# First-batch keys and queries loaded by three tokens per partition, patterns copied by transfers, and a new order of work

## The chip, the cores and the metric

The kernel runs on one core of one Trainium2 chip. The metric is the time of one execution on the device in microseconds; the time before is 271.98 us, the median of three runs between 271.74 and 272.3 us. The engines are named as the profile names them: PE (matmul; PEld is its weight load), DVE (VectorE), ACT (ScalarE), POOL (GpSimd), SP (SyncE, which here only issues transfers); 16 DMA engines move the data.

## The reference

Inputs q, k and v have the shape [4, 8, 768, 64] (batches, heads, tokens, width), w_in is [512, 2048], w_out [2048, 512], all fp32. First comes an attention that selects chunks of 32 keys:

```python
k_min, k_max = min and max of k over each chunk of 32 keys          # 24 chunks
ub = np.sum(np.maximum(q * k_min, q * k_max), axis=-1)              # a bound for each query and chunk
ub = np.where(chunk is not in the future, ub, -1e9)
top_chunks = np.argsort(ub, axis=-1)[..., -6:]
mask = (chunk of key in top_chunks) & (query position >= key position)
attn = softmax(np.where(mask, q @ k.T / 8, -1e9));  x = attn @ v    # x: [3072, 512] over all heads
```

Then a dense part on the 3072 tokens: `h = x @ w_in`, `g = h * clip(h + 3, 0, 6) / 6`, and the result is `g @ w_out`, [3072, 512] in fp32.

## The kernel before

The work is cut by batch (four), by half of the tokens (384), and by two pairs of heads: sixteen units of two pairs each, n = 0 to 15. Units 0 to 3 are the first batch. For each unit the keys and queries are put in order (width down the partitions), the chunks' limits are reduced on DVE, PE makes the bounds (`bounds`, L442), DVE takes the six largest of each query and makes a mask of them, and PE multiplies queries and keys (`scores`). ACT takes the exponential, POOL cuts the triangle, and PE multiplies with the values (`values`, tile PVP). When a half of a batch has all its heads, its tokens are turned (XT) and go through the dense part: PE `hidden` (L587, tile HP), ACT and DVE (tiles U and GT), PE `result` (L602, tile OP).

The first batch is treated unlike the others. Its keys and queries come as they lie in memory, a token per partition (`load_quad`); each (pair, half) is turned by PE into PSUM with three fp32 transposes against an identity (`turn`, L375, tiles KT and QT), and copied out by ACT or DVE (`turn_out`). The later batches are loaded in blocks of 32 (`load`, L237) and turned by DVE. In the first batch the mask is a matmul of its own with a pattern tile EB; in the later batches a copy of EB lies beside the keys in the same tile KL, and `beside` makes that copy for six KL buffers and two heads each, on DVE, ACT or POOL, whichever is free.

The order of the instructions on each engine is written out by a planner (`class Plan`). Every step is added with an engine, a length, a rank, the steps it comes after, and the buffers it takes and gives. `order` then plays the program through in time by these lengths, picking on every engine the ready step of the lowest rank, and the program is written in that order; each engine then works strictly in that order on the chip. The table SHIFT moves the rank of single steps by their number. The tables RANK, BEHIND (how long after a step's end others may use it) and GATE (after which landed input each half of a weight matrix is loaded) steer it further. All input loads of the first batch are issued by SP and, in part for unit 0, by ACT; SEQ gives their order: K0 Q0 K1 Q1 Q3 Q2 K2 V1 V0 V2 K3 V3. At most eight transfers (lanes) are under way at once. The weights come through POOL's queue in four parts, WIN in two and WOUT in two (`load_weights`, L316 and L319); a tiny read of the gating input goes before each. In the first 45 us, where the plan leaves PE idle, `occupy` issues bf16 matmuls with no use (L365) into spare columns of the bank of the step just issued, to keep PE at work.

Of the kernel before, what the change touches and what calls it, by code (L numbers as in the profile page):

```python
# [48 lines left out]
class Plan:  # L49
# [5 lines left out]

    BEHIND = dict(PE=0.24, ACT=0.15, DVE=0.15, POOL=0.15, SP=0.3, DMA=0.9, GEN=0.0, WT=1.2)
    COLD = 6.5

# [4 lines left out]
    def add(self, engine, length, rank, run=None, after=(), take=(), give=(), port=False, tiles=None, lock=None):  # L63


        step = dict(lengths=engine if isinstance(engine, dict) else {engine: length}, rank=(rank + SHIFT.get(len(self.steps), 0), len(self.steps)),
                    run=run, told=isinstance(engine, dict), port=port, tiles=tiles, lock=lock, take=take, give=give, then=[])
# [26 lines left out]
    def order(self, **busy):  # L94

        free = {e: busy.get(e, 0.0) for e in self.BEHIND}
        port, tiles, locks = dict(DVE=0.0, POOL=0.0), None, {}
# [17 lines left out]
        while events:  # L115
            now, _, done, own = heapq.heappop(events)
            if done:
                behind(done, own)
                if not own:
                    for held in done["give"]:  # L120
                        held[1] -= 1
                        if not held[1]:
                            self.room[held[0]].append(held[2])
            for e, steps in ready.items():
                if free[e] > now + 1e-9:
                    continue
                for st in sorted(steps, key=lambda x: x["rank"][:1] if e == "DMA" else x["rank"]):
# [4 lines left out]
                    elif self.room_for(st):  # L132
                        steps.remove(st)
                        for held in st["take"]:
                            held[2] = self.take(held[0])
                        out.append(st)
# [11 lines left out]
                        if e == "DMA":  # L148
                            weights = max(free["WT"] - now, 0.0) + sum(x["lengths"]["WT"] for x in ready["WT"])
                            length = min(length / 0.15, weights + max(length - 0.15 * weights, 0.0))  # L150
# [18 lines left out]
def kernel(  # L169
# [36 lines left out]

    def bank(name, shape, dtype=FP32):
        return ps_mix.tile(shape, dtype, name=name, tag=tag("m"))
# [65 lines left out]
    for name, x in (("KS", k), ("QS", q)):  # L274
        for part in range(4):
# [58 lines left out]
    def beside(i, j, e):  # L334

        copy(e, KLS[i][OTHER[j], j, :], EB[OTHER[j], i % 2, :])
# [24 lines left out]
    spare = []  # L361

    def occupy(times):
        for _ in range(times):
            nc.tensor.matmul(spare[-1], lhsT=IDENTB[:], rhs=IDENTB[:, 0:spare[-1].shape[-1]], start=True, stop=True)  # L365

    def turn(st, name, half):

        if st["b"] == 0:
            x = st[name][:, half, :, st["own"], :]  # L370
            T = bank(name[0] + "T", [P, HS + P])
            spare.append(T[:, HS:])
            T = st[name, half] = T[:, 0:HS]
            for t in range(HB):
                nc.tensor.transpose(T[:, t * P:(t + 1) * P], x[:, t, :, :], IDENT32[:])  # L375
# [54 lines left out]
    def bounds(us):  # L430
        for u in us:
            T = bank("UBT", [P, HS + P])
            spare.append(T[:, HS:])
            u["UBT"] = T[:, 0:HS]
# [50 lines left out]
    def scores(st, half, t):  # L485
        SP = st["SP", half, t] = ps_score.tile([P, 2, 512], FP32, name="SPS", tag=tag("s"))
        for jb, q0, n, c0 in PLAN[half][t]:
# [31 lines left out]
    def values(st, half):  # L519
        if (st["b"], half) not in X_tiles:  # L520
            X_tiles[st["b"], half] = xpool.tile([P, HB, DMODEL], BF16, name="Xb", tag=tag("x"))
        T = bank("PVP", [P, HS + P])
        spare.append(T[:, 2 * HB * (D + 1):])
        PVP = st["PVP", half] = T[:, 0:2 * HB * (D + 1)].rearrange("p (j n d) -> p j n d", j=2, n=HB)
# [114 lines left out]
    GATE = dict(I0="V2", I1="I0", O0="I1", O1="O0")  # L639
# [15 lines left out]
    def arrive(engine, issue, length, run, after=(), take=(), parts=1):  # L655
# [3 lines left out]
        for part in range(parts):  # L659
# [6 lines left out]
            if engine == "POOL":  # L666
                issued.append(got)
                got = add("GEN", 1.2, 0, after=[got])
            landed.append(add("WT" if engine == "POOL" else "DMA", length, 0, after=[got], give=lane))
# [4 lines left out]
    def load_input(n, name, after=()):  # L674
# [6 lines left out]
        if n == 0:  # L681
            plan.room[name.lower()].remove(0)
            held_inputs[name, 0][2] = 0
            for i, st in enumerate(two):
                lanes = [hold("lane", 1, 4 * (name == "QS") + 2 * i + j) for j in range(2)]
                for lane in lanes:
                    plan.room["lane"].remove(lane[2])
                there[name, st["pair"], 0] = [add("DMA", 1.0 if name == "KS" else 1.15, i + 2 * (name == "QS") - 10, give=lanes)]
        elif n < 4:
            there[name, two[0]["pair"], half] = there[name, rest, half] = [  # L690
                *arrive("SP", 0.52, 0.6, (load_quad, n, name, x), take=take, parts=3,
                        after=[first_issue[1, name]] if n == 3 else [])]
# [20 lines left out]
    for what in SEQ.split():  # L713
# [5 lines left out]
        else:  # L719
            load_input(n, name)  # L720
            landing[what] = there[name, units[n][0][0]["pair"], units[n][1]], lambda n=n, name=name, at=at: units[n][0][0][name][0:1, units[n][1], at, 3, 0:1]
# [14 lines left out]
    def prepare(n):  # L736
# [11 lines left out]
        for st in two:  # L748
# [3 lines left out]
            for name, f in (("KS", "kf"), ("QS", "qf")):  # L752
# [3 lines left out]
                if first:  # L756
                    m = bank_of[name] = hold("m", 2 if name == "KS" else 1)
                    here = direct[name] = [add("PE", 0.34, r + lead, later(turn, st, name, half), after=here, take=[m], give=used)]
# [232 lines left out]
```

## Time and profile before

| | |
|---|---|
| median of three runs | 271.98 us |
| the profiled execution, as timed | 271.37 us |
| its span, first to last instruction | 269.7 us |
| PE busy | 256.8 us (95%) |
| DVE busy | 209.4 us (78%) |
| ACT busy | 191.6 us (71%) |
| POOL busy | 128.7 us (48%) |
| moved by DMA | 33.71 MB in 122720 packets, 113216 of them under 512 bytes |
| granted clock of PE | 1.000 |

A line of a group names the line of the code, the engine, the operation, the output and input tiles, the shape and the count, then the busy time and the mean of one, and the idle time of the engine before these instructions with what ended it. PE's busy time overlaps itself: a matmul is counted to the end of its way through the array, while the next one has begun. [...]

### The profile page before, as it was taken

The numbers are of one execution on the slowest core, as the hardware profiler recorded it, in microseconds if no ns is written. First come the engines' busy times: TensorE is split into PE (matmuls) and PEld (weight loads), VectorE is DVE, ScalarE is ACT, GpSimd is POOL, SyncE is SP. The second block draws the span as 40 slices with busy tenths as digits, with TensorE's granted clock in tenths as the row PEclk, the third lists the DMA queues.
The fourth block names the chain that finished last, engine by engine and source line by source line (L and its number), as shares of the span: only waits on it lengthen the run. The fifth ranks groups of instructions, "written<-read, shape, count | busy, mean of one in ns | idle before, by whom it ended". The sixth has DMA issues, their size and how long they took to land.

```text
span 269.7 us, 6517 instructions
## 1 busy us (share of the span) xinstructions
PE 256.8 (95%) x2350; PEld 152.7 (57%) x2373; DVE 209.4 (78%) x588; ACT 191.6 (71%) x306; POOL 128.7 (48%) x289
## 2 busy tenths in 40 slices
PE   7997999898999999999999999999999999999994
PEld 4645565654445677644664566654665756555443
DVE  7799898989799997899989999999894424857000
ACT  3589899685527899765984499953998874868021
POOL 4168579533767485559734666752842310200000
PEclk9999999999999999999999999999999999999999
DMA  8999999999948999954995599114103003201122
GB/s 166 219 198 188 190 175 154 176 149 185 212 108 117 127 157 176 186 164 139 150 159 141 157 155 181 40 60 139 39 4 117 5 38 139 58 0 41 39 78 79
DMA packets 122720, 33.71 MB, mean 125 GB/s; under 512 B 113216, under 2 KB 118080, under 8 KB 122688
## 3 DMA queue, kind: packets, MB, share of 16 engines
q1 hardware_dynamic: 117952, 28.71, 62.2%
q0 software_dynamic: 3136, 4.19, 9.5%
q10 hardware_dynamic: 1600, 0.39, 0.7%
q8 instruction: 18, 0.29, 0.6%
q14 instruction: 14, 0.11, 0.2%
HBM read 29.23 MB, written 8.26 MB: 139 GB/s over the span
## 4 chain that ended last, share of the span: by engine, by line
PE 73%; DMA 10%; DVE 8%; SPq 4%; ACT 2%; issue 1%; ACTq 0%; DVEq 0%
PE OP L602 28%; PE HP L587 23%; PE SPS L497 9%; DMA KS<-in_k_dram 8%; PE PVP L530 6%; PE UBT L442 4%; SPq L229 2%; DVE GT L595 2%; PE SPS L494 2%; DMA VS<-in_v_dram 2%; ACT PT L507 1%; PE OP L610 1%; SPq L237 1%; DVE KMA L401 1%; DVE KMA L400 1%
## 5 line engine op out<-in xcount | busy, mean ns | idle before, releaser
L587 PE MATMUL HP<-XT,WIN 128*128 128x384 bf16 x512 | 92.4, 326 | 2.4 <-DVE GT L595 2.3
L507 ACT ACTIVATE PT<-SPS 128x1024 bf16<-128x1024 f32 (+1 forms) x96 | 85.3, 927 | 12.0 <-PE SPS L497 9.9
L602 PE MATMUL OP<-WOUT,GT 128*128 128x512 bf16 x345 | 82.3, 379 | 1.9 <-issue 0.5
L592 ACT ACTIVATE U<-HP,THREE 128x384 bf16<-128x384 f32 x128 | 73.0, 594 | 15.1 <-PE HP L587 8.8
L595 DVE SCALAR_TENSOR_TENSOR GT<-U,HP 128x384 bf16<-128x384 bf16 x128 | 67.2, 545 | 14.9 <-ACT U L592 11.0
L587 PEld LDWEIGHTS <-WIN 128*128 128x128 bf16 x512 | 48.5, 98 | 34.4 <-issue 4.0
L602 PEld LDWEIGHTS <-GT 128*128 128x128 bf16 x368 | 35.1, 98 | 40.2 <-issue 3.7
L512 POOL TENSOR_SCALAR_AFFINE_SELECT PT<-PT 128x256 bf16<-128x256 bf16 x96 | 38.9, 418 | 35.9 <-ACT PT L507 34.9
L497 PE MATMUL SPS<-QLA,KL 128*128 128x384 bf16 (+2 forms) x240 | 36.3, 278 | 0.0
L628 ACT ACTIVATE OT<-OP 128x512 f32<-128x512 f32 x22 | 13.1, 597 | 27.4 <-PE OP L602 27.0
L331 POOL TENSOR_SCALAR_AFFINE_SELECT KL<-KF 64x384 bf16<-64x384 f32 x48 | 23.9, 501 | 14.4 <-DVE KF L387 12.1
L331 POOL TENSOR_SCALAR_AFFINE_SELECT QLA<-QF 64x384 bf16<-64x384 f32 x48 | 24.6, 512 | 12.2 <-DVE QF L387 6.3
L497 PEld LDWEIGHTS <-KL 128*128 128x128 bf16 x240 | 21.7, 98 | 12.8 <-issue 0.6
L530 PEld LDWEIGHTS <-PT 128*128 128x128 bf16 x672 | 23.9, 97 | 3.1 <-issue 0.4
L530 PE MATMUL PVP<-VB,PT 128*128 128x65 bf16 x672 | 25.6, 194 | 0.0
L411 ACT ACTIVATE QR<-QF 128x384 f32<-128x384 f32 x30 | 15.4, 531 | 9.4 <-DVE QF L387 9.3
L542 DVE TENSOR_TENSOR Xb<-PVP,RINV 128x384 bf16<-128x384 f32 x32 | 18.5, 579 | 1.1
L580 POOL COPY XT<-BF 128x384 bf16<-128x384 bf16 x20 | 9.3, 504 | 16.7 <-DMA BF<-BD 16.6
L536 DVE RECIPROCAL RINV<-PVP 128x6 f32<-128x6 f32 x32 | 5.9, 185 | 12.6 <-PE PVP L530 12.2
L387 DVE STREAM_TRANSPOSE KF<-KS 128x384 f32<-128x384 f32 x24 | 13.2, 560 | 1.7 <-DMA KS<-in_k_dram 1.3
L387 DVE STREAM_TRANSPOSE QF<-QS 128x384 f32<-128x384 f32 x24 | 12.8, 555 | 2.0 <-DMA QS<-in_q_dram 2.0
L400 DVE TENSOR_REDUCE KMA<-KF 128x12 f32<-128x384 f32 x24 | 13.1, 545 | 0.4
(80 smaller groups left out, 235.8 us busy)
## 6 DMA issues: line engine op xcount, KB each, us to landing
out_dram<-OT SPq DMA_DIRECT2D x23, 256.0 KB, 2.3
KS<-in_k_dram SPq DMA_DIRECT2D x24, 192.0 KB, 5.5
QS<-in_q_dram SPq DMA_DIRECT2D x24, 192.0 KB, 6.5
VT<-in_v_dram SPq DMA_DIRECT2D x24, 192.0 KB, 4.5
WIN<-in_moe_w_in_dram POOLq DMA_DIRECT2D x2, 1024.0 KB, 9.4
WOUT<-in_moe_w_out_dram POOLq DMA_DIRECT2D x2, 1024.0 KB, 10.1
BD<-BT SPq DMA_DIRECT2D x5, 384.0 KB, 2.4
BF<-BD SPq DMA_DIRECT2D x20, 96.0 KB, 2.3
```

Source lines behind the costliest of these rows:

```text
L331: nc.gpsimd.affine_select(out=to, in_=x, pattern=[[0, n]], compare_op=A.is_ge, fill=0.0, base=0, channel_multiplier=0)
L387: nc.vector.transpose(T[:], st[name][:, st["i"], half * HC:(half + 1) * HC, :].rearrange("p c e -> p (c e)"))
L400: nc.vector.tensor_reduce(out=over, in_=chunks, axis=X_AXIS, op=A.max)
L497: nc.tensor.matmul(SP[:, j, c0:c0 + n], lhsT=KLS[st["pair"] % 6][:, j, jb * P:(jb + 1) * P], rhs=st["QL", half][:, j, at:at + n], start=Tr ...
L507: nc.scalar.activation(PT[:, :, 0:cols], SP[:, :, 0:cols], ACT.Exp, scale=scale)
L512: nc.gpsimd.affine_select(out=PT[:, :, c0:c0 + P], in_=PT[:, :, c0:c0 + P], pattern=[[0, 2], [1, P]], compare_op=A.is_ge, fill=0.0, base=0 ...
L530: nc.tensor.matmul(PVP[:, j, n, :], lhsT=PT[:, j, c0:c0 + P], rhs=st["VB"][:, jb, j, :], start=(jb == 0), stop=(jb == qb))
L542: nc.vector.tensor_tensor(out=to, in0=PVP[:, :, :, 0:D], in1=RINV[:].to_broadcast([P, 2, HB, D]), op=A.mult)
L587: nc.tensor.matmul(HP[:], lhsT=WIN[:, kt, f * P:(f + 1) * P], rhs=g["XT"][:, kt, :, :], start=(kt == 0), stop=(kt == KT_HID - 1))
L592: nc.scalar.activation(U[:], g["HP", f][:], ACT.Relu, bias=THREE[:], scale=1.0)
L595: nc.vector.scalar_tensor_tensor(out=g["GT"][:, f, :], in0=g["U", f][:], scalar=6.0, in1=g["HP", f][:], op0=A.min, op1=A.mult)
L602: nc.tensor.matmul(g["OP", t][:], lhsT=g["GT"][:, f, t * P:(t + 1) * P], rhs=WOUT[:, f, :], start=(f == 0), stop=(f == FT - 1))
```

## The change

1. `load_quad`: three neighbouring tokens go to one partition, so that a piece of a transfer is 3 x 64 fp32 values (768 bytes) where it was one token (256 bytes). A load of one unit's keys or queries is two transfers, one for each pair of heads (192 KB each), where it was three (four for unit 0, of 96 KB). A pair's steps wait for its own transfer alone. Unit 0's second transfer is issued by ACT.
2. `turn`: with three tokens on a partition the columns come out in another order, which a transpose does not mend. Six ordinary fp32 matmuls per turn take their place: for each token t of three and each head j of the pair, 64 columns of data are the stationary operand and the identity is the moving one; the result is written into every third column of 64 partitions.
3. `beside`: the twelve copies of EB become transfers that SP issues, from SBUF to SBUF.
4. The matmuls without use stand ahead of a step, in the bank that the step itself will write, after the bank has come free, up to 24 of them, by the idle time that the plan saw before the step (`occupied`).
5. The planner: other lengths and delays for transfers (`share`, BEHIND, FETCH), WIN's first half gated by V3, WOUT's first half by the keys of the second batch (K4), WOUT's second half by WIN's second half; and a new SHIFT table, by which every engine's order differs.

The diff without SHIFT, which is replaced as a whole, and without the lines that only pass new lengths:

```diff
-            two[0][name] = two[1][name] = src_pool.tile([P, 2, HB, 4, D], FP32, name=name, tag=tag(name.lower()))
-        to, x = two[0][name][:, half], heads(x, two[0]).rearrange("j (n p) d -> p n j d", p=P)[:, half * HB:half * HB + HB, :, :]
-        if n == 0:
-            (nc.scalar if part % 2 else nc.sync).dma_start(to[:, :, part], x[:, :, part])
-        else:
-            nc.sync.dma_start(to[:, part], x[:, part])
+            two[0][name] = two[1][name] = src_pool.tile([P, 2, 4, HB, D], FP32, name=name, tag=tag(name.lower()))
+        own = two[part]["own"]
+        (nc.scalar if n == 0 and part else nc.sync).dma_start(
+            two[0][name][:, half, own], heads(x, two[0])[own, half * HS:(half + 1) * HS].rearrange("j (p t) d -> p j t d", t=HB))
...
-    def beside(i, j, e):
-
-        copy(e, KLS[i][OTHER[j], j, :], EB[OTHER[j], i % 2, :])
+    def beside(i, j):
+
+        nc.sync.dma_start(KLS[i][OTHER[j], j, :], EB[OTHER[j], i % 2, :])
...
-            x = st[name][:, half, :, st["own"], :]
-            T = bank(name[0] + "T", [P, HS + P])
-            spare.append(T[:, HS:])
-            T = st[name, half] = T[:, 0:HS]
+            x = st[name][:, half, st["own"]]
+            T = st[name, half] = bank(name[0] + "T", [P, HS])
             for t in range(HB):
-                nc.tensor.transpose(T[:, t * P:(t + 1) * P], x[:, t, :, :], IDENT32[:])
+                for j in range(2):
+                    nc.tensor.matmul(T[:].rearrange("p (n t) -> p n t", t=HB)[64 * j:64 * j + 64, :, t], lhsT=x[:, j, t, :], rhs=IDENT32[:], start=True, stop=True)
...
-    GATE = dict(I0="V2", I1="I0", O0="I1", O1="O0")
+    GATE = dict(I0="V3", I1="I0", O0="K4", O1="I1")
...
-            made["EB", p % 6] = [add(dict(DVE=0.52, ACT=0.81, POOL=0.85), None, r + RANK["eb"], later(beside, p % 6, j), port=True, after=free.get(("KL", p - 6), []))
-                                 for j in range(2)]
+            made["EB", p % 6] = []
+            for j in range(2):
+                lane = hold("lane")
+                issue = add("SP", 0.42, r + RANK["eb"], later(beside, p % 6, j), after=free.get(("KL", p - 6), []), take=[lane])
+                made["EB", p % 6].append(add("DMA", 0.4, 0, after=[issue], give=[lane], share=0.27))
...
+    def occupied(T):
+        for _ in range(idle.pop(0) if idle else 0):
+            nc.tensor.matmul(T[:, 0:P] if len(T.shape) == 2 else T[:, 0, 0, 0:D], lhsT=IDENTB[:], rhs=IDENTB[:, 0:D if len(T.shape) > 2 else P], start=True, stop=True)
+        return T
...
+        idle[:] = []
+        if step["engine"] == "PE" and step["at"] < 45 and step["idle"] > 0.3 + 0.2 * bool(step["tiles"]):
+            idle[:] = [min(24, int((step["idle"] - 0.1 - 0.2 * bool(step["tiles"])) * 0.8 / 0.058))]
```

More of the change, by code (lines that the diff above doesn't have):

```diff
@@ L27 @@
 SHIFT = {
[18 rows of a table removed]
[16 rows of a table added]
 }
 class Plan:
-    BEHIND = dict(PE=0.24, ACT=0.15, DVE=0.15, POOL=0.15, SP=0.3, DMA=0.9, GEN=0.0, WT=1.2)
+    BEHIND = dict(PE=0.24, ACT=0.15, DVE=0.15, POOL=0.15, SP=0.3, DMA=0.7, GEN=0.0, WT=1.2)
     COLD = 6.5
+    FETCH = 15.3, 1.35
     def __init__(self, **room):
@@ L96, in order @@
         free = {e: busy.get(e, 0.0) for e in self.BEHIND}
-        port, tiles, locks = dict(DVE=0.0, POOL=0.0), None, {}
+        port, tiles, locks, opened = dict(DVE=0.0, POOL=0.0), None, {}, {}
         ready = {e: [] for e in self.BEHIND}
@@ L135, in order @@
                             held[2] = self.take(held[0])
+                        st["idle"] = now - max([free[e], *(opened.get((held[0], held[2]), 0.0) for held in st["take"])])
                         out.append(st)
@@ L274 @@
     for name, x in (("KS", k), ("QS", q)):
-        for part in range(4):
+        for part in range(2):
             load_quad(0, name, x, part)
@@ L667, in arrive @@
                 issued.append(got)
-                got = add("GEN", 1.2, 0, after=[got])
-            landed.append(add("WT" if engine == "POOL" else "DMA", length, 0, after=[got], give=lane))
+                got = add("GEN", 1.0, 0, after=[got])
+            landed.append(add("WT" if engine == "POOL" else "DMA", length, 0, after=[got], give=lane, share=0.1 if length > 1 else 0.18 if run[0] is load_quad else 0.15))
         return landed
@@ L684, in load_input @@
             for i, st in enumerate(two):
[L685 to L688, printed above, removed]
+                lane = hold("lane", 1, plan.lane)
+                plan.room["lane"].remove(plan.lane)
+                plan.lane += 1
+                there[name, st["pair"], 0] = [add("DMA", 1.1 if name == "KS" and i == 0 else 0.65, i + 2 * (name == "QS") - 10, give=[lane])]
         elif n < 4:
-            there[name, two[0]["pair"], half] = there[name, rest, half] = [
-                *arrive("SP", 0.52, 0.6, (load_quad, n, name, x), take=take, parts=3,
-                        after=[first_issue[1, name]] if n == 3 else [])]
+            got = arrive("SP", 0.52, 0.65, (load_quad, n, name, x), take=take, parts=2, after=[first_issue[1, name]] if n == 3 else [])
+            there[name, two[0]["pair"], half], there[name, rest, half] = got[:1], got[1:]
         elif half == 0:
@@ L720 @@
             load_input(n, name)
-            landing[what] = there[name, units[n][0][0]["pair"], units[n][1]], lambda n=n, name=name, at=at: units[n][0][0][name][0:1, units[n][1], at, 3, 0:1]
+            landing[what] = there[name, units[n][0][1]["pair"], units[n][1]], lambda n=n, name=name, at=at: units[n][0][0][name][0:1, units[n][1], 3, at, 0:1]
     vs = hold("gt", 2 * H // 2, 1)
@@ L948 @@
             a = add("SP", 0.37, -2000, later(result_out, g, t, nc.sync), after=[a], take=[lane])
-            add("DMA", 0.75, 0, after=[a], give=[ot, lane])
+            add("DMA", 0.75, 0, after=[a], give=[ot, lane], share=0.4)
         r += RANK["step"]
-    for step in (steps := plan.order(PE=3.7, ACT=4.25, DVE=4.4, POOL=3.2, SP=3.7, DMA=1.6, WT=1.6)):
+    for step in plan.order(PE=3.7, ACT=4.25, DVE=4.4, POOL=3.2, SP=1.9, DMA=1.6, WT=1.6):
         chosen = {}
@@ L954 @@
             chosen.setdefault(kind, []).append(number)
-        spare.clear()
+        idle[:] = []
+        if step["engine"] == "PE" and step["at"] < 45 and step["idle"] > 0.3 + 0.2 * bool(step["tiles"]):
+            idle[:] = [min(24, int((step["idle"] - 0.1 - 0.2 * bool(step["tiles"])) * 0.8 / 0.058))]
         if step["run"]:
             step["run"](*[step["engine"]] if step["told"] else [])
-        if spare:
-            end = step["at"] + step["length"]
-            idle = min(other["at"] for other in steps if other["engine"] == "PE" and other["at"] > step["at"]) - end
-            if end < 45 and idle > 0.25:
-                occupy(min(16, int((idle - 0.2) * 0.8 / 0.058)))
 _INS = ['q', 'k', 'v', 'moe_w_in', 'moe_w_out']
```

34 lines of the change are left out of this document (16 added, 18 removed), and 34 rows, old and new, of the table SHIFT.

## The prediction

> **What bounds the kernel now.** I read the busy times by stage first, then TensorE's instructions in the first stages, then the chain that ended last, then the transfers. The stages (columns: the stretch and its length, busy time and instructions of PE, weight loads, DVE, ACT and POOL, granted clock, DMA share, GB/s):
>
> ```profile
> 0.00:35.60 35.60, 30.60 (x363) 19.32 (x363) 29.86 (x108) 25.82 (x43) 18.90 (x50) 1.00 1.12 191
> 35.60:80.00 44.40, 41.65 (x389) 22.92 (x388) 39.82 (x90) 30.78 (x52) 26.68 (x55) 1.00 1.14 169
> 80.00:266.10 186.10, 184.59 (x1603) 110.47 (x1622) 139.72 (x391) 134.37 (x210) 83.16 (x185) 1.00 0.57 103
> 10.00:15.00 5.00, 4.22 (x48) 3.36 (x46) 4.33 (x18) 3.79 (x8) 1.26 (x4) 1.00 1.29 220
> 122.00:123.00 1.00, 0.95 (x6) 0.41 (x6) 1.00 (x3) 0.54 (x2) 0.93 (x4) 1.00 0.67 182
> ```
>
> After 80 us PE is busy for 184.59 of 186.1 us: nothing to win there but by fewer matmuls. Earlier its busy time flatters, since a matmul's modelled duration overlaps the next one's. So I count matmuls and price them by their spacing where they run back to back. The counts, up to the first dense matmul at 35.6 us and up to 80 us:
>
> ```profile
> L494 PE MATMUL SPS<-MT,EB 64*128 64x384 bf16 (+2 forms) x56 | 7.4, 276 | 2.6 <-ACT PT L507 2.0 <-DVE MT L472 0.5
> L494 PE MATMUL SPS<-KL 64*128 64x384 bf16 (+2 forms) x56 | 6.6, 273 | 0.0
> L375 PE MATMUL QT<-IDENT,QS 128*128 128x128 f32 x24 | 4.3, 300 | 0.3 <-DMA QS<-in_q_dram 0.3
> L375 PE MATMUL KT<-IDENT,KS 128*128 128x128 f32 x24 | 4.3, 315 | 0.5 <-DMA KS<-in_k_dram 0.5
> L442 PE MATMUL UBT<-QF,KMA 64*32 64x384 f32 x32 | 4.0, 495 | 0.1
> L442 PE MATMUL UBT<-QR,KMA 64*32 64x384 f32 x32 | 3.9, 486 | 0.1
> L530 PE MATMUL PVP<-VB,PT 128*128 128x65 bf16 x78 | 3.1, 194 | 0.0
> ```
> ```profile
> L587 PE MATMUL HP<-XT,WIN 128*128 128x384 bf16 x128 | 23.4, 326 | 2.2 <-DVE GT L595 2.1
> L602 PE MATMUL OP<-WOUT,GT 128*128 128x512 bf16 x42 | 9.9, 379 | 0.6 <-DVE GT L595 0.4 <-issue 0.2
> L530 PE MATMUL PVP<-VB,PT 128*128 128x65 bf16 x168 | 6.3, 194 | 0.0
> ```
>
> The spacings, from the chain that ended last (start, length, what) and from the timeline of PE:
>
> ```profile
> 11.87 0.54 SPq L243
> ...
> 13.04 4.84 DMA VS<-in_v_dram
> 17.90 0.56 DVE VB L255
> ...
> 33.92 0.78 PE XTP L551 x12
> 34.70 0.98 PE SPS L494 x16
> ...
> 38.38 0.91 PE PVP L530 x30
> ...
> 71.74 0.86 PE OP L602 x4
> 72.61 1.45 PE UBT L442 x32
> 74.22 4.26 PE OP L602 x19
> ...
> 139.56 3.90 PE HP L587 x24
> ```
> ```profile
> 10.31 0.87 PE L375 MATMUL QT<-IDENT,QS 128*128 128x128 f32 x6
> ...
> 16.60 0.85 PE L442 MATMUL UBT<-QF,KMA 64*32 64x384 f32 x8
> ...
> 17.27 0.82 PE L442 MATMUL UBT<-QR,KMA 64*32 64x384 f32 x8
> ```
>
> Useful PE time up to 35.6 us: 112 x 0.061 (0.98/16) = 6.8 for the first batch's scores, 16 turns of three transposes x 0.43 (0.87/2) = 6.9, four bounds x 1.5 = 6.0, 78 x 0.030 = 2.4, 12 x 0.065 = 0.8: 22.9. So 12.7 us of this stage hold no useful matmul. From 35.6 to 80: 128 x 0.1625 = 20.8, 42 x 0.215 = 9.0, the remaining 90 of PVP 2.7, and some 6.6 for the rest of the scores (48 x 0.061), two joint bounds (2 x 1.45) and 12 turns of tokens (0.8): 39.1, so 5.3 are empty. Together 18 us, and only there can this change win.
>
> What holds PE in those stages: the chain runs through SP's issues to V's transfer (13.04), and from 17.90 through DVE to 28 us. DVE is busy 29.86 of the first 35.6 us, ACT 25.82; of the idle rest, 5.7 and 9.8, some 1.3 and 4.2 lie before anything has landed, so 4.4 and 5.6 count.
>
> **The change, part by part.**
>
> *Loads.* The first batch's K and Q (3.1 MB) go in pieces of 768 bytes for 256. Near 10 us only 256-byte pieces move: 220 GB/s at a share of 1.29, or 171 per unit of share. At 122 us it is the words fetched back (96 KB over 32 partitions and four groups, 768 bytes a piece): 182 at 0.67, or 272. At 0.63 of the engine time per byte, 3.1 MB cost some 9.0 us instead of 14.3: an estimate of 5.3 us of transfer time freed, between 0 (if the piece size isn't what counts) and that. SP issues 18 of these loads ahead of the first V (11.87); there will be 12 if V keeps its place, at 0.54 each 3.2 us sooner; the bytes ahead of V would allow 4.6. I take V 3.2 us earlier. It doesn't become 3.2 us of time: next in line is DVE, with those 4.4 idle us, and nothing takes its reductions away. The gain lies between 0 and 4.4; I take the middle, 2.2.
>
> *Turns.* Three fp32 transposes become six fp32 matmuls of 64 columns. The bounds show what an ordinary fp32 matmul costs: each stands twice in the trace (x64 for 32 in the code), and a group with four column tiles moves 384 columns in 0.33 us per step (17.27 - 16.60, two steps), so 128 columns take 0.11. If the two halves of a turn run side by side as the bounds' column tiles do, a turn is six steps, 0.66 + 0.1, or 0.33 us more than now; 16 of them 5.3 us. Otherwise it is twelve steps, 1.42, and 15.8 us more in all. Nearest is the bounds' row: paired. PE's 12.7 empty us (3.4 before the first turn) cover it except where a turn is itself waited for: the first unit's last K and last Q, 0.7 us. Ends: 0 and 2.6 (eight turns).
>
> A rule of the Trainium skill speaks against this part: "TensorEngine Tiling" (Key Properties) says that a change of tiling mode drains the array, and each turn is now a 128x64 island among 128x128 work. The chain shows it once: bounds at 72.61 end at 74.06, the next OP begins at 74.22, so 0.16 us; by the rule 16 turns cost some 2.6 us more, of which the two turns on the path would be 0.3, and the forecast would be 269.2.
>
> *Patterns.* Twelve copies leave three engines (busy, mean, idle before):
>
> ```profile
> L257 POOL TENSOR_SCALAR_AFFINE_SELECT KL<-EB 64x768 bf16<-64x768 bf16 x6 | 5.1, 844 | 2.7 <-DVE IDENTB L301 1.7 <-PE SPS L494 0.8
> ...
> L253 ACT COPY KL<-EB 64x768 bf16<-64x768 bf16 x3 | 2.5, 822 | 0.0
> L255 DVE COPY KL<-EB 64x768 bf16<-64x768 bf16 x3 | 1.4, 462 | 0.0
> ```
>
> 9.0 us of engine time. Four of the twelve stand before 6 us in the timeline, in idle time; two of ACT's stand at 31.3 and 36.3 us among exponentials that PE waits for (0.82 each). I take 0.3, ends 0 and 1.6. In exchange SP gets 12 issues (6.5 us against 8 x 0.54 = 4.3 saved) and the DMA engines 1.2 MB, 3.4 us at the 768-byte rate (182/0.67 x 1.29 = 350 GB/s), 5.4 at 220. So the freed transfer time is given back by the time the second batch is loaded. They aren't needed before its scores at 79.9 us, which hides them; without that cover they would delay the second batch's loads by those 3.4 to 5.4 us.
>
> *Weights and order.* The weight loads now form a file, each issued when the one before has landed:
>
> ```profile
> 24.89 1.00 POOL L316 DMA_DIRECT2D WIN<-in_moe_w_in_dram  x1
> ...
> 34.53 0.77 POOL L316 DMA_DIRECT2D WIN<-in_moe_w_in_dram  x1
> 45.54 0.93 POOL L319 DMA_DIRECT2D WOUT<-in_moe_w_out_dram  x1
> 55.94 0.92 POOL L319 DMA_DIRECT2D WOUT<-in_moe_w_out_dram  x1
> ```
>
> With the new gates the first WOUT half waits for K of the second batch (issued by 27.9 us), so it follows the second WIN half by one issue; the last half follows that WIN half's landing, about 45.5 instead of 55.94. Both WOUT halves then share the engines: complete between 56 and 65.5 us (ten for one half each, side by side or in line), against 66 now. So OP matmuls can fill PE up to 10 us sooner, at least 0. Of the 5.3 empty us of that stage I take a third, 1.7, with ends 0 and 5.3. WIN's first half, moved from V2 to V3, waits for a later transfer in a shorter queue: V3 is last of the first batch, and 4.6 us sooner it comes about when V2 does now. Cost 0.
>
> *Fillers.* The 42 matmuls without use now go in front of a step in its own bank, up to 24 x 0.056 = 1.3 us at a place. Where data come sooner than the plan thinks, they delay the step. I take 0.4 lost, ends 0 and 2.
>
> Sum: 2.2 - 0.7 + 0.3 + 1.7 - 0.4 = 3.1 us off the profiled execution's 271.37 us (span 269.7). That lies 0.6 below the median of 271.98, so the forecast for the median is **268.9 us**.
>
> **The rivals.**
>
> *Hidden anyway.* DVE and ACT set the first 35.6 us, V lands sooner and waits, and the turns take back the rest. For it: DVE has no gap over 0.2 us from 17.9 to 25 us in the chain. Against: ACT has 5.6 idle us there. Gain 0.6 (the patterns and a little of the weights): 271.4.
>
> *Both holes close.* DVE's 4.4 and half of the second stage's 5.3, less 0.7: 6.3 off, 265.7.
>
> *The second batch starves (slower).* With weight loads back to back, the 128-byte loads of K and Q get what is left. For it: the timeline of SP already shows one unit's four Q issues held for 13.23 us beside the first WIN half.
>
> ```profile
> 27.98 13.23 SPq L237 DMA_DIRECT2D QS<-in_q_dram  x4
> ```
>
> Against: 96 OP matmuls belong to the first batch, of which 54 are left at 80 us, 11.6 us of PE work, and the gain of 3.1 uses part of it. It decides from 8.5 us of delay to the second batch's Q; each further us costs one. Were the eight loads from 41 us on put off until 57, they would run 13 us late and cost 4.5: 273.4. "DMA: Bandwidth & Descriptors" of the Trainium skill (Queues, rings and completion order) has each DMA engine take its queues in turn by whole packets; the 13.23 us agree with a small share for the small pieces.
>
> *The turns don't pair (slower).* 15.8 us more PE time against 9.3 empty ones: 6.5 over, 275.4. The bounds' row speaks against it.
>
> **How the numbers follow.** Forecast 48 in 100, own range 267.0 to 270.8 (its parts at half and at one and a half). Both holes 12, hidden 17, starving 16, no pairs 7. A change of 0.2% (0.54 us) is about what can be told here. Faster: 48 + 12 + 9 of the hidden case = 69; same 7 of it; slower 16 + 7 + 1 = 24. From 266.0 to 273.8 leaves out the unpaired case, a quarter of the starving one and half of the closed holes, some 17 in 100.
>
> **What the changed profile would show.** KS and QS issues of 192 KB each with about 3 us to landing and GB/s above 260 before 12 us; first V issue near 8.5 us; 192 fp32 matmuls in the turns, pairs starting within 10 ns, 0.75 us a turn; no KL<-EB on POOL, ACT or DVE and 12 issues on SP; the first HP at about 34 instead of 35.68; the last WOUT issue near 44; empty PE time under 15 us before 80. The prediction is wrong if HP's start hasn't moved, if a turn takes over 1 us, or if PE waits for KF or QF of the second batch between 60 and 85 us.

## The result and the profile after

The changed kernel takes 270.86 us (median of 19 runs, 269.63 to 272.19) where the kernel before, run beside it, takes 272.47 us (19 runs, 271.19 to 274.07): a ratio of 0.9933, 95% interval 0.9913 to 0.9953. That is 0.7% faster, a small change, but the interval leaves out 1. The forecast was 268.9 us and a faster kernel. The profiled execution took 270.71 us, its span is 269.0 us; against the profiled execution of before (271.37) it is only 0.7 us shorter, since that one lies 1.1 us under its median of this day.

The stages of the kernel after (columns as in the prediction), cut at its first dense matmul, at 80 us, and three short stretches:

```profile
0.00:34.40 34.40, 31.59 (x466) 21.48 (x466) 27.84 (x105) 24.01 (x41) 17.64 (x47) 1.00 1.03 212
34.40:80.00 45.60, 45.39 (x415) 25.35 (x417) 40.74 (x99) 33.84 (x57) 22.71 (x51) 1.00 1.13 185
80.00:265.40 185.40, 181.55 (x1588) 108.38 (x1602) 136.66 (x380) 131.78 (x209) 85.21 (x187) 1.00 0.56 102
5.00:10.00 5.00, 5.00 (x94) 4.83 (x94) 3.59 (x9) 3.98 (x9) 2.19 (x4) 1.00 1.11 326
80.00:120.00 40.00, 37.32 (x373) 23.87 (x375) 33.94 (x96) 30.63 (x45) 26.13 (x57) 1.00 0.99 143
84.00:96.00 12.00, 11.31 (x142) 7.76 (x141) 8.92 (x23) 10.24 (x13) 7.33 (x18) 1.00 1.14 134
```

The same stretches of the kernel before:

```profile
5.00:10.00 5.00, 5.00 (x49) 3.48 (x49) 3.24 (x9) 2.03 (x5) 0.98 (x2) 1.00 1.27 215
80.00:120.00 40.00, 39.51 (x398) 25.23 (x410) 35.65 (x108) 33.66 (x50) 24.04 (x55) 1.00 1.07 156
84.00:96.00 12.00, 11.89 (x106) 7.21 (x105) 11.16 (x38) 10.94 (x15) 8.03 (x19) 1.00 1.40 139
```

The first loads do what was forecast of them: 326 GB/s at a DMA share of 1.11 between 5 and 10 us, against 215 at 1.27. That is 294 GB/s per unit of share against 169, or 0.58 of the engine time per byte where the forecast had 0.63. The new thing is in the last rows. After 80 us, where the kernel before had PE busy for 39.51 of 40 us, it is now busy for 37.32, and DVE for 8.92 of the 12 us from 84 on, where it was 11.16.

PE's groups after, the turns up to 34.4 us and the dense part from there to 80 us:

```profile
L377 PE MATMUL KT<-IDENT,KS 128*64 128x128 f32 x96 | 6.7, 289 | 0.2 <-DMA KS<-in_k_dram 0.2
L377 PE MATMUL QT<-IDENT,QS 128*64 128x128 f32 x96 | 6.2, 275 | 0.0
...
L586 PE MATMUL HP<-XT,WIN 128*128 128x384 bf16 x128 | 22.0, 326 | 0.0
L601 PE MATMUL OP<-WOUT,GT 128*128 128x512 bf16 x63 | 14.3, 379 | 0.2 <-issue 0.2
```

192 matmul records are turns, 12 for each of the 16; and 63 OP matmuls stand before 80 us where there were 42, which is 21 x 0.215 = 4.5 us of work done sooner. The chain that ended last shows the price of a turn (x12), and what PE and DVE hang on after 83 us (start, length, what):

```profile
7.97 0.66 PE KT L377 x12
...
34.47 1.41 PE HP L586 x8
...
63.01 0.21 PE OP L601
...
84.64 0.60 ACT OT L627
...
85.25 0.33 SPq L633
...
88.22 5.51 DMA KS<-in_k_dram
...
93.81 0.59 DVE KF L389
```

A result tile is scaled by ACT (OT), SP issues its store (L633), and only then the keys behind it in SP's queue (L246), which DVE must turn (KF). The timeline of SP shows the stop, after and before:

```profile
76.64 8.95 SPq L633 DMA_DIRECT2D out_dram<-OT  x3
85.68 3.75 SPq L246 DMA_DIRECT2D KS<-in_k_dram  x4
```
```profile
76.55 6.40 SPq L634 DMA_DIRECT2D out_dram<-OT  x2
83.05 3.59 SPq L237 DMA_DIRECT2D KS<-in_k_dram  x4
```

Three stores instead of two stand directly ahead of the third batch's keys, and SP stands still from 80.14 to 85.25 us for the last of them. So the keys are issued 2.6 us later than before, while PE arrives sooner. The list of waits of 83 to 118 us shows what that costs DVE, of after and of before (total us, times, longest):

```profile
DVE KF L389 <- DMA KS<-in_k_dram: 3.3, 2, 2.4
```
```profile
DVE KF L387 <- DMA KS<-in_k_dram: 0.6, 1, 0.6
```

To see where time is won and lost I add up PE's useful matmuls by the time they start, at the prices of the prediction (turns and matmuls of no use left out; all of it is 239.7 us). It is worked out from all rows of each trace; a few OP matmuls have no record and are counted by their weight loads. Its last two columns belong to experiments below.

| us of useful PE work by | before | after | keys first | keys first, casts on POOL |
|---|---|---|---|---|
| 35 us | 14.7 | 15.3 | 14.6 | 14.8 |
| 80 us | 54.7 | 59.5 | 58.5 | 58.9 |
| 100 us | 74.8 | 77.9 | 77.8 | 78.2 |
| 120 us | 94.5 | 95.7 | 97.8 | 98.4 |
| profiled execution | 271.37 | 270.71 | 268.22 | 267.76 |

After is 0.6 us ahead at 35 us, 4.8 at 80, and only 1.2 at 120: 0.6 from the first stage (loads, turns and order together), 4.2 from the second, and 3.6 given back. These are single executions. With the keys first the program is the same as after up to 70 us, and yet its execution stands 0.7 us lower at 35 and 0.9 at 70 us (48.8 against 49.7): so early differences under 1 us are at the edge of what one execution tells. From 80 to 120 us the columns do 39.8, 36.2, 39.3 and 39.5 us of work, and that difference is far outside it.

### The profile page after: what moved, and what is told of

It reads as the page before. It is cut to its first block, busy times and chain, and to the rows that moved or that the text cites. A ratio compares the mean times of both kernels' runs of the same rounds, so it can differ in the third digit from the quotient of the medians.

```text
span 269.0 us, 6720 instructions
## 1 busy us (share of the span) xinstructions
PE 258.5 (96%) x2466; PEld 155.2 (58%) x2484; DVE 205.2 (76%) x582; ACT 190.0 (71%) x305; POOL 125.6 (47%) x284
## 4 chain that ended last, share of the span: by engine, by line
PE 73%; DVE 8%; DMA 7%; ACT 4%; SPq 3%; issue 1%; POOL 1%; ACTq 0%; DVEq 0%; POOLq 0%
PE OP L601 24%; PE HP L586 23%; PE SPS L498 6%; DMA KS<-in_k_dram 5%; PE PVP L529 5%; PE UBT L442 5%; PE SPS L495 3%; DVE GT L594 3%; ACT PT L508 3%; PE QT L377 2%; PE KT L377 2%; SPq L246 2%; PE OP L609 1%; DVE KF L389 1%; DMA BD<-BT 1%
## 5 line engine op out<-in xcount | busy, mean ns | idle before, releaser
L508 ACT ACTIVATE PT<-SPS 128x1024 bf16<-128x1024 f32 (+2 forms) x96 | 84.5, 927 | 11.6 <-PE SPS L498 7.9
L586 PE MATMUL HP<-XT,WIN 128*128 128x384 bf16 x512 | 90.1, 326 | 1.3 <-DVE Xb L541 0.8
L601 PE MATMUL OP<-WOUT,GT 128*128 128x512 bf16 x350 | 83.4, 379 | 1.2 <-issue 0.3
L591 ACT ACTIVATE U<-HP,THREE 128x384 bf16<-128x384 f32 x128 | 71.6, 594 | 8.1 <-PE HP L586 4.2
L586 PEld LDWEIGHTS <-WIN 128*128 128x128 bf16 x512 | 48.8, 98 | 32.6 <-issue 1.3
L513 POOL TENSOR_SCALAR_AFFINE_SELECT PT<-PT 128x256 bf16<-128x256 bf16 x96 | 39.6, 423 | 51.5 <-ACT PT L508 50.7
L498 PE MATMUL SPS<-QLA,KL 128*128 128x384 bf16 (+2 forms) x240 | 35.5, 278 | 0.1
L340 POOL TENSOR_SCALAR_AFFINE_SELECT KL<-KF 64x384 bf16<-64x384 f32 x48 | 24.1, 504 | 8.3 <-DVE KF L389 6.7
L529 PE MATMUL PVP<-VB,PT 128*128 128x65 bf16 x672 | 26.3, 193 | 1.2 <-POOL PT L513 1.1
L413 ACT ACTIVATE QR<-QF 128x384 f32<-128x384 f32 x29 | 14.5, 525 | 10.4 <-DVE QF L389 8.5
L541 DVE TENSOR_TENSOR Xb<-PVP,RINV 128x384 bf16<-128x384 f32 x32 | 18.5, 579 | 1.1
L579 POOL COPY XT<-BF 128x384 bf16<-128x384 bf16 x20 | 9.7, 523 | 14.9 <-DMA BF<-BD 14.8
L266 POOL TENSOR_SCALAR_AFFINE_SELECT VB<-VT 128x768 bf16<-128x768 f32 x12 | 10.8, 908 | 6.4 <-DMA VT<-in_v_dram 4.3
```

Of the source, the lines that this page charges most:

```text
L340: nc.gpsimd.affine_select(out=to, in_=x, pattern=[[0, n]], compare_op=A.is_ge, fill=0.0, base=0, channel_multiplier=0)
L413: nc.scalar.activation(QR[:], QF[:], ACT.Relu)
L498: nc.tensor.matmul(SP[:, j, c0:c0 + n], lhsT=KLS[st["pair"] % 6][:, j, jb * P:(jb + 1) * P], rhs=st["QL", half][:, j, at:at + n], start=Tr ...
L508: nc.scalar.activation(PT[:, :, 0:cols], SP[:, :, 0:cols], ACT.Exp, scale=scale)
L513: nc.gpsimd.affine_select(out=PT[:, :, c0:c0 + P], in_=PT[:, :, c0:c0 + P], pattern=[[0, 2], [1, P]], compare_op=A.is_ge, fill=0.0, base=0 ...
L529: nc.tensor.matmul(PVP[:, j, n, :], lhsT=PT[:, j, c0:c0 + P], rhs=st["VB"][:, jb, j, :], start=(jb == 0), stop=(jb == qb))
```

## The experiments

Ratios are to the kernel before, run beside each; the changed kernel's is 0.9933. The medians of the kernel before beside the experiments lie between 272.58 and 273.31 us, so differences in us against 270.86 are uncertain by up to 0.8 us.

### The third batch's keys before the store

```diff
-    for step in plan.order(PE=3.7, ACT=4.25, DVE=4.4, POOL=3.2, SP=1.9, DMA=1.6, WT=1.6):
+    steps = plan.order(PE=3.7, ACT=4.25, DVE=4.4, POOL=3.2, SP=1.9, DMA=1.6, WT=1.6)
+    number = [step["rank"][1] for step in steps]
+    store = steps.pop(number.index(1126))
+    steps.insert([step["rank"][1] for step in steps].index(400) + 1, store)
+    for step in steps:
```

Step 1126 is the third of those stores, step 400 the last of the four key loads.

> The changed kernel with one result's store, for which SP stands still from 80.1 to 85.25 us, moved behind the four key loads of the third batch that stand behind it. If the gain that PE had at 80 us (4.8 us of work ahead of the kernel before) is lost up to 115 us because DVE waits for these keys, the loads are issued near 80 us, the waits of DVE for KS (3.3 us) go, and 1.5 to 3 us come back: 268 to 269.4. If it is lost because the dense work that filled PE there has been used up earlier, the time doesn't move by more than 0.5 us.

Measured: 268.42 us (267.6 to 268.68), ratio 0.9838 [0.9806, 0.987], faster than both kernels. Its SP timeline and its stretch from 80 to 120 us:

```profile
76.57 4.77 SPq L633 DMA_DIRECT2D out_dram<-OT  x2
81.43 3.69 SPq L246 DMA_DIRECT2D KS<-in_k_dram  x4
```
```profile
80.00:120.00 40.00, 39.91 (x436) 24.83 (x415) 36.63 (x103) 33.81 (x51) 28.73 (x62) 1.00 1.05 153
```

The keys go out 4.25 us sooner, PE is busy for 39.91 of 40 us, and DVE's wait for KS is no longer in the list. From 80 to 120 us it does 39.3 us of useful work, where after did 36.2. One instruction's place in one queue was worth 2.4 us: this cause is shown.

### The loads by 256-byte pieces again

```diff
-        own = two[part]["own"]
-        (nc.scalar if n == 0 and part else nc.sync).dma_start(
-            two[0][name][:, half, own], heads(x, two[0])[own, half * HS:(half + 1) * HS].rearrange("j (p t) d -> p j t d", t=HB))
+        to, x = two[0][name][:, half], heads(x, two[0])[:, half * HS:(half + 1) * HS].rearrange("j (t p) d -> p j t d", t=HB)
+        for t in ((0, 1), (2,))[part]:
+            (nc.scalar if n == 0 and part else nc.sync).dma_start(to[:, :, t], x[:, :, t])
...
-                    nc.tensor.matmul(T[:].rearrange("p (n t) -> p n t", t=HB)[64 * j:64 * j + 64, :, t], lhsT=x[:, j, t, :], rhs=IDENT32[:], start=True, stop=True)
+                    nc.tensor.matmul(T[:].rearrange("p (t n) -> p n t", t=HB)[64 * j:64 * j + 64, :, t], lhsT=x[:, j, t, :], rhs=IDENT32[:], start=True, stop=True)
```

> The changed kernel with the first batch's keys and queries in 256-byte pieces again (one token per partition, three transfers a unit); order, turns and everything else stay as changed. If the larger pieces pay through earlier inputs, as the forecast has it, the time rises by 2 to 4 us over the changed kernel's 270.86, V's first issue moves 3 us later and the first dense matmul to 36 or 37 us. If DVE and ACT hide the transfers anyway, the time stays within 0.6 us.

Measured: 278.27 us (277.82 to 279.25), ratio 1.0208 [1.0178, 1.0238], 7.4 us over after, more than the most that the loads' term allowed (4.4). PE's longest wait, and its stretches:

```profile
PE KT L377 <- DMA KS<-in_k_dram: 4.2, 2, 3.9
```
```profile
5.00:10.00 5.00, 4.02 (x60) 3.04 (x62) 2.30 (x6) 2.85 (x6) 1.01 (x2) 1.00 1.36 218
10.00:15.00 5.00, 1.07 (x16) 0.83 (x14) 0.56 (x1) 0.00 (x0) 1.64 (x2) 0.67 1.36 218
15.00:20.00 5.00, 5.00 (x52) 3.33 (x50) 1.96 (x5) 2.48 (x5) 0.51 (x1) 0.65 1.10 200
```

218 GB/s again, and with the order kept PE and DVE stand nearly still from 10 to 15 us (1.07 and 0.56 us busy), since each works strictly in the written order and the next instruction in line waits for its data. The granted clock was 0.67 and 0.65 in these two stretches on top. So this prices "late data in an order drawn for early data", not the part alone.

### Loads and turns of before, in the order of after

```diff
-        own = two[part]["own"]
-        (nc.scalar if n == 0 and part else nc.sync).dma_start(
-            two[0][name][:, half, own], heads(x, two[0])[own, half * HS:(half + 1) * HS].rearrange("j (p t) d -> p j t d", t=HB))
+        to, x = two[0][name][:, half], heads(x, two[0])[:, half * HS:(half + 1) * HS].rearrange("j (t p) d -> p t j d", t=HB)
+        for t in ((0, 1), (2,))[part]:
+            (nc.scalar if n == 0 and part else nc.sync).dma_start(to[:, t], x[:, t])
...
-                for j in range(2):
-                    nc.tensor.matmul(T[:].rearrange("p (n t) -> p n t", t=HB)[64 * j:64 * j + 64, :, t], lhsT=x[:, j, t, :], rhs=IDENT32[:], start=True, stop=True)
+                nc.tensor.transpose(T[:, t * P:(t + 1) * P], x[:, t, :, :], IDENT32[:])
...
```

> The changed kernel's order, gates, patterns by SP and fillers, with the loads in 256-byte pieces and the three fp32 transposes of the kernel before. Loads alone as before took 278.27. If the two parts add up, the turns' 5.3 us come off: 273. If with late inputs PE has room for the dearer turns, they cost less there: 276 to 278. Against 270.86 it says what loads and turns are worth together in this order; the forecast made it 1.5 us.

Measured: 276.81 us (276.12 to 277.57), ratio 1.0142 [1.0114, 1.017]. Loads and turns are as before (a unit's load is three transfers, for unit 0 too); order, patterns, gates and fillers are new, and it is 3.9 us slower than the kernel before. So these without the new loads and turns are a loss; the order is good only with the arrivals that it was drawn for.

### Both kernels without their SHIFT tables

The edit is `SHIFT = {}` in each.

> The changed kernel with an empty SHIFT table, so that its order is the planner's plain one by ranks. To be read against the kernel before with an empty table, which runs beside it. Theory: the parts of the change (loads, turns, patterns by SP, gates) are themselves worth 1 to 3 us, and the rest of what undoing one of them cost (5.5 to 7.4 us) is that the tuned order had been drawn for them: both kernels lose 2 to 8 us without their tables, and this one is 1 to 3 us ahead of the other. Rival: a part is worth in any order what undoing it cost, and then this one is 5 us or more ahead. Second rival: the parts are worth nothing and the new table alone earned the 1.6 us: this one is level with the other or behind it.

> The kernel before with an empty SHIFT table. Theory: 2 to 8 us over the kernel before, a ratio of 1.007 to 1.03, and 1 to 3 us over the changed kernel with an empty table; by the rival 5 us or more over that; by the second rival level with it or under it.

Measured: after 280.5 us (279.93 to 281.3), ratio 1.0286 [1.0245, 1.0326]; before 280.42 us (276.88 to 282.85), 1.031 [1.0219, 1.0401]. The medians are level, but those of before differ in clock: 276.88 us at a granted clock of 1.000, 278.74 at 0.994, 282.09 at 0.986, 282.85 at 0.988. At the full clock after took 279.93 and 280.02, some 3 us more than the one such run of before. So the second rival holds, level or behind. Where it is lost shows in PE's busy time from 80 to 120 us, of after and of before:

```profile
80.00:120.00 40.00, 34.44 (x336) 20.81 (x335) 31.38 (x96) 30.78 (x49) 23.47 (x52) 1.00 1.03 143
```
```profile
80.00:120.00 40.00, 39.57 (x416) 24.74 (x415) 37.14 (x113) 31.78 (x48) 24.48 (x57) 1.00 0.98 146
```

Counted as in the table, after is some 5 us of useful work ahead at 80 us here too, and some 2 us behind at 120. So the parts do gain before 80 us in the plain order as well, and more than that gain is lost behind it. DVE's wait for the third batch's keys isn't among the waits there; the most that PE waits there is 2.3 us, for POOL (PT). What is behind that loss stays open, and so does the price of the parts apart from the table.

### Turns twice

```diff
-            for t in range(HB):
+            for t in [*range(HB), *range(HB)]:
```

> The changed kernel with each turn's matmuls made twice (the same result written again): 192 fp32 matmuls more, 16 x 0.66 = 10.6 us of PE in the first 30 us. If the turns are mostly hidden in PE's empty time, as the forecast has it, only what doesn't fit into some 5 empty us shows: 4 to 6 us more than 270.86. If the turns are the chain at the start, as the changed kernel's chain reads (turn after turn from 4.0 to 9.9 us), nearly all of it shows: 8 to 11 us more.

Measured: 281.18 us (280.95 to 282.19), ratio 1.0317 [1.0288, 1.0347], 10.3 us over after. The work added is 192 matmuls, 16 x 0.66 = 10.6 us:

```profile
L377 PE MATMUL KT<-IDENT,KS 128*64 128x128 f32 x192 | 13.2, 300 | 0.3 <-DMA KS<-in_k_dram 0.3
L377 PE MATMUL QT<-IDENT,QS 128*64 128x128 f32 x192 | 11.5, 274 | 0.0
```

Nearly all of it shows: no empty PE time takes up more turning.

### Turns at half the price

```diff
+            flat = st[name][:, half, st["own"]].rearrange("p j t d -> p (j t d)")
             for t in range(HB):
-                for j in range(2):
-                    nc.tensor.matmul(T[:].rearrange("p (n t) -> p n t", t=HB)[64 * j:64 * j + 64, :, t], lhsT=x[:, j, t, :], rhs=IDENT32[:], start=True, stop=True)
+                nc.tensor.transpose(T[:].rearrange("p (n t) -> p n t", t=HB)[:, :, t], flat[:, t * P:(t + 1) * P], IDENT32[:])
```

> The changed kernel with its loads and its order, but three 128-column fp32 transposes per turn, as before, over the wrong columns (the heads and tokens of a pair come out mixed, so the selection and the result are of other data; the amount of work is the same otherwise). A turn falls from 0.66 to 0.33 us of PE. If a turn's time lies on the path from start to first dense work, as doubling it showed (10.6 us of work added cost 10.3), 16 x 0.33 = 5.3 us go: about 265.6. If the first half of a turn's cost is hidden, as the forecast has it, only 0.7 us go: 270.2.

Measured: 269.91 us (268.11 to 271.25), ratio 0.9885 [0.9828, 0.9941]. Its four runs differ by the granted clock: 268.11 us at 1.000, 269.81 at 0.991, 270.01 at 0.992, 271.25 at 0.987. With less turning PE runs empty for a while, and in three of the four its clock was lower; the profiled one shows both:

```profile
20.00:25.00 5.00, 2.42 (x37) 1.63 (x33) 4.93 (x20) 4.12 (x7) 4.07 (x9) 0.91 0.94 153
25.00:30.00 5.00, 5.00 (x68) 2.62 (x64) 3.20 (x8) 3.15 (x4) 1.59 (x5) 0.75 1.22 211
```

At the full clock half the turning is worth 270.86 - 268.11 = 2.7 of 5.3 us, by a single run; with the lower clock, by the median, 1.0. As far as that one run tells, the dearer turns cost about 2.7, at the far end of the term's 0 to 2.6.

### Turns without a change of tiling mode

The same edit, with `nc.tensor.matmul(..., lhsT=flat[:, t * P:(t + 1) * P], rhs=IDENT32[:], start=True, stop=True)` in place of the transpose: PE's time as in after, in full 128x128 tiles.

> The changed kernel with three ordinary 128-column fp32 matmuls per turn over the wrong columns (result of other data, as in the run with transposes): the same 0.66 us of PE, but no change of tiling mode around a turn. If a change of mode costs the 0.16 us that one place of the chain before shows, 16 turns are 2.6 us cheaper: 268.3 where all of it is on the path. If it costs nothing here, 270.9 within 0.5.

Measured: 271.10 us (270.14 to 272.49, 8 runs), ratio 0.9938 [0.9918, 0.9958], that of after. 16 turns that no longer change the tiling mode bring nothing here (the two ratios differ by 0.0005, 0.1 us). "TensorEngine Tiling (Array Packing)" of the Trainium skill (Key Properties) has a change of tiling mode drain the array. The 2.6 us that the prediction weighed by that rule aren't there.

### Patterns copied by POOL

```diff
-        nc.sync.dma_start(KLS[i][OTHER[j], j, :], EB[OTHER[j], i % 2, :])
+        copy("POOL", KLS[i][OTHER[j], j, :], EB[OTHER[j], i % 2, :])
```

> The changed kernel with the twelve pattern copies on POOL, at the same places in the order, instead of SP's transfers. If the copies cost something because engines are short of time, 12 x 0.84 = 10 us more on POOL show as 0.3 to 1.6 us of time. If POOL has room where they now stand (8 to 13 us and 67 to 74 us), nothing changes within 0.5 us, and SP's queue is 6 us shorter.

Measured: 276.39 us (275.83 to 276.55), ratio 1.0131 [1.0106, 1.0155], 5.5 us over after and outside both expectations. PE's longest wait after 36 us and the chain:

```profile
PE UBT L442 <- POOL KMA L405: 2.9, 1, 2.9
```
```profile
83.65 0.20 POOL KMA L405
...
83.90 0.83 PE UBT L442 x4
...
89.54 0.60 ACT OT L627
90.16 0.33 SPq L633
...
90.58 0.38 SPq L246
...
93.04 5.58 DMA KS<-in_k_dram
```

Eight of the copies, 0.82 us each, stand at 65 to 80 us on POOL, the limits (KMA) behind them, PE's bounds (UBT) behind these, then the result tile, the store, and the third batch's keys, issued 4.9 us later than in after. The chain thus runs through the same store; how much of the 5.5 us that is isn't measured. The copies of the kernel before stood at 3.9 to 49.5 us on three engines, and what they cost there isn't measured by this either.

### Weights by the gates of before

```diff
-    GATE = dict(I0="V3", I1="I0", O0="K4", O1="I1")
+    GATE = dict(I0="V2", I1="I0", O0="I1", O1="O0")
```

> The changed kernel with the gates of the weights as before (WIN's first half after V2, WOUT's halves each after the part before them); the planner draws up the order anew with the same ranks. If the earlier WOUT is what fills PE between 35 and 80 us, WOUT's last issue moves from 43 to about 53 us, PE has some 1.7 us more empty time before 80 us, and the time rises by 1 to 3 us. If order and early inputs are all, it stays within 1 us.

Measured: 277.82 us (275.61 to 277.89), ratio 1.0159 [1.0117, 1.0202]. That is more than either expectation had. The planner drew another order for these gates, so the 7 us are of gates and order together. Useful PE work by 80 us is 57.4, 2.1 less than in after. It doesn't price the gates.

### Without the matmuls of no use

```diff
-        for _ in range(idle.pop(0) if idle else 0):
+        for _ in range(0):
```

> The changed kernel without its matmuls of no use. The trace shows nine of them, 0.5 us in all. By the prediction's term they cost 0.4 us where data come sooner than the plan thinks: then this is 0.2 to 0.6 us faster than the changed kernel, a ratio to before near 0.992. Rival: they keep the granted clock up in the first 40 us, and without them the clock in the rows falls and the time is over 1 us longer, a ratio over 0.997. If neither, they cost and bring nothing: within 0.2 us.

Measured: 270.52 us (270.24 to 271.73), ratio 0.9918 [0.9881, 0.9956]. That can't be told from no change: they cost 0.3 us or nothing. The granted clock was 0.999 or 1.000 in five of the six runs without them (0.992 in one), so they don't keep it up.

### Keys first, and two casts from ACT to POOL

```diff
+        if step["rank"][1] in (271, 129):
+            step["engine"] = "POOL"
```

> The changed kernel with the store put behind the third batch's keys (as in the run before that did this), and two casts of the first batch's values, which stand at about 22 us on ACT, given to POOL at the same places of the order; nothing else differs. Theory: what is left in the first 35 us is ACT's time, since PE waits there some 1.1 us for exponentials and ACT spends 2 x 0.53 us on these casts among them; the gain then stays, because nothing after 80 us takes it back any more: 0.3 to 0.8 us less than with the keys first alone, a ratio to before of 0.981 to 0.983. Rival: POOL's casts of 0.54 us delay the triangles behind them, which the values' matmuls wait for, and the two cancel: a ratio of 0.984 or more. Either way the ratio should stay under 0.990; over that, the gain from putting the keys first was not real.

Measured: 267.40 us (267.09 to 267.76), ratio 0.9804 [0.9772, 0.9836], the fastest here. In its first 36 us PE waits 0.9 us for a mask (DVE MT) where with the keys first alone it waited 1.2 us for exponentials, and the table has it 0.4 us ahead of that run at 80 us and 0.6 at 120. The intervals of the two overlap; the sign is likely, the size isn't settled.

## Why the prediction was right and wrong

*The sign and its places held.* Transfers of 768 bytes go faster, V is issued at 7.35 us (forecast near 8.5), a turn is six steps and 0.66 us, the first dense matmul starts at 34.47 (about 34) and the last WOUT half is issued at 43.12 (about 44). PE's waits before 80 us shrink. Empty PE time before 80 us fell under the 15 us that were forecast: 59.5 us of useful work and 10.6 of turns leave 9.9. Two signs were met in part: the first loads landed after 3.1 to 4.9 us (about 3), and the closest starts within a turn are 6 or 7 ns apart in half of the cases and 17 or 18 in the others (within 10). The median is 2.0 us over the forecast, inside the wide range (266.0 to 273.8) and 0.06 us over the range of its main case (267.0 to 270.8).

*Loads and turns, 2.2 - 0.7 = 1.5.* PE is 0.6 us ahead at 35 us in the profiled execution, and level in that with the keys first: less than half of the 1.5. The step that failed is "PE's 12.7 empty us ... cover it": the turns at half price say 2.7 us at the full clock (one run), not 0.7, and turns made twice added nearly their whole price. Empty time summed over a stage isn't cover, since part of it lies where PE waits for DVE and ACT, and each turn has its place in a chain. That the loads then gave some 3 us gross is worked out from the 0.6 and the 2.7, not measured.

*Weights and order, 1.7.* The second stage gave 4.2, so the upper end (5.3) was nearer than the third that I took: OP matmuls did fill PE, 63 against 42 by 80 us. How much of it is the gates and how much the order stays open.

*Patterns, 0.3.* Not measured as such. That the second batch's scores hide them held: PE's waits name no KL<-EB.

*Fillers, 0.4.* 0.3 or nothing: the size fits, but it can't be told from zero. Only nine of them are in the changed kernel's trace, 42 in that of before.

*"After 80 us ... nothing to win there".* This is the step that missed the time. It is true of winning and was taken for "nothing to lose"; the sum ended at 80 us. PE was full there as long as the third batch's keys came in time (DVE waited 0.6 us for them). The kernel after reaches that point 4.8 us sooner with the keys 2.6 later, and gives back 3.6 by 120 us. Putting the keys first returns 2.4 us of it.

*Luck.* The time lies in the range because two errors work against each other: 4.8 us gained by 80 us where the sum had 3.1, and 3.6 lost behind it where the sum had nothing. That 268.42 us with the keys first is so near the 268.9 of the forecast is luck as well, since the terms of the first two stages were off by 0.9 and 2.5 us in opposite directions.

*The rivals.* By the time alone, 1.6 us gained lies between the 0.6 of "hidden anyway" and the 3.1 of the forecast. That rival comes near in the first stage, which gained 0.6 us, but it has nothing like the 4.2 us of the second. The starving rival had the kind of wait, but looked for it one batch too early, and in bandwidth instead of in the order of one queue. SP was in fact held 20.60 us over three key issues of the second batch (from 34.44 us, beside the weights), and PE still waited for none of that batch's keys or queries between 60 and 85 us.

## What to carry to other kernels

When work moves ahead, look behind the stage that gains: what arrives just in time there can arrive late afterwards, and an engine that is full before the change may not stay full after it. In a queue that issues strictly in order, a store that waits for an engine holds every load behind it; find the long row of that queue's timeline and see what stands after it. Taking one part out of a kernel whose order was tuned for it measures the order too, not the worth of the part: undoing the loads costs 7 us in the tuned order, while all the parts together bring no shorter time in the plain one.

## What the runs showed of the hardware

The granted clock answered the same idle time in different ways. PE ran no matmul from about 10.5 to 14.4 us both with the 256-byte pieces and with the loads and turns of the kernel before in the new order; these stretches are of the first and of the second:

```profile
11.00:12.00 1.00, 0.00 (x0) 0.00 (x0) 0.00 (x0) 0.00 (x0) 1.00 (x2) 0.84 1.37 219
12.00:13.00 1.00, 0.00 (x0) 0.00 (x0) 0.00 (x0) 0.00 (x0) 0.39 (x1) 0.50 1.36 217
...
17.00:18.00 1.00, 1.00 (x12) 0.46 (x12) 0.30 (x1) 0.75 (x2) 0.00 (x0) 0.50 1.28 225
18.00:19.00 1.00, 1.00 (x12) 0.31 (x8) 0.00 (x0) 0.71 (x2) 0.51 (x1) 0.75 0.87 171
```
```profile
12.00:13.00 1.00, 0.00 (x0) 0.00 (x0) 0.00 (x0) 0.00 (x0) 0.42 (x1) 1.00 1.36 217
```

In the first the clock was halved at about 11.7 us (0.84 is two thirds of that microsecond at 1.00 and the rest at 0.50), some 1.2 us after the last matmul, and stayed so until about 18.5 us, 4 us after work had come back; in the second it never fell. "TensorE: Matmul & The Clock Gate" of the Trainium skill (Part 1) has half the clock after at least one idle window of about 3.4 us that runs on its own. The halved value agrees, but the moment doesn't: the clock fell before 3.4 us without a matmul had passed. The half-price turns show the same: no matmul from 22.0 to 24.5 us, and the clock at 0.50 from about 24.1 us, some 2.1 us in. What decided between falling and not falling stays open.

A DMA share over 1.0 doesn't need two queues. From 5 to 10 us in the run with the 256-byte pieces only SP's queue has packets in the trace, and the share is 1.36, so packets of the one queue overlap in time.
